# Bucketed attention and two feed-forward layers: another order of the first units, of the weight loads and of the drain

## The chip, the cores and the metric

One NeuronCore of one Trainium2 chip runs the whole kernel. The metric is the device time of one execution, in microseconds (us). The kernel before took 798.04 us, the median of three runs (796.69 to 798.05).

## What is computed

```python
# q, k, v: (2 batches, 8 heads, 768 tokens, 64), proj: (64, 6), all float32
q_bucket = sum((q @ proj > 0) * 2**bit); k_bucket likewise
scores = where(q_bucket == k_bucket, q @ k.T / 8, -1e9)
attn = softmax(scores) @ v
x = attn, heads joined: 1536 tokens x 512
# twice: w_in (512, 2048), w_out (2048, 512); the weights arrive as float64
h = x @ w_in;  g = h * clip(h + 3, 0, 6) / 6;  x = g @ w_out       # first layer
h = x @ w_in2; g = h * tanh(softplus(h));      out = g @ w_out2    # second layer
```

## The kernel before

**Attention.** Two heads of a batch form a pair; there are 8 pairs. A unit is 128 queries of one head against its 768 keys, so a pair has 12 units, and there are NU = 96. `attention_step(n)` (L657) is called with n = 0, 2, 4, ... and works on three generations at once: the scores S of units n and n+1 (`emit_S`, L565, into the PSUM tiles s0 and s1), the transposes T of units n-6 and n-5 (`emit_T`, L607, into the banks t0 and t1) and the product with V of units n-12 and n-11 (`emit_pv`, L626). TensorE gets them in the order PV, PV, T, S, T, S. Between S and T a unit passes through a minimum over its keys on VectorE (L581), the exponential on ScalarE (L587), four small statistics for four units together (L592, in every second step) and the normalization on GpSimd (L604). Each half of a transpose is taken out of its bank by ScalarE (L468) or VectorE (L469) before the next transpose may use that bank.

**A pair's preparation.** Scores need each operand in a high and a low float32r part, and the bucket bits as 12 more rows. The first pair is prepared straight into place (`k_hi`, `k_lo`, `q_hi`, `q_lo`, `q_dup`, `bits_out`, with `first_z` for the bucket products of TensorE), partly ahead of step 0 and partly in `late_prep` (L545), which is called right after step 0. A later pair p is prepared in stages by `prep(p, s)` (L476) at the ends of the steps of the pair before: the bucket products (`prep_z`, L425), the high parts kh and qh on GpSimd (L486), the scaled bits on GpSimd (L487) and the low part of q on VectorE (L489), then copies by DMA (`move`, L471) into the operand tiles KA, QA, QB, KX, the low part of k on GpSimd (L505) with its copies, and the load of pair p+1. For the second pair (p = 1) every stage stands one step later.

**Weights.** A weight unit is 512 KB of float64, loaded into one of five buffers (`w_load`, L104) and decoded into two float32r parts by some ten VectorE and ScalarE operations (L125 to L168) that `w_push` spreads over three calls. The first five loads are issued after step n = 4. The first decoding operation is a ScalarE one (L135) in step n = 18.

**Drain.** From n = 96 there are no more scores. The last six steps hold the last transposes (n = 96, 98 and 100) and products with V; after each step come the first matmuls of the feed-forward layer (`moe_pe(i)`: h of block i, and y of block i-2), two `w_push` calls, and the parts of g of a block (`g_parts`, L271: a ReLU on ScalarE, the gate on VectorE, the high part on ScalarE, the low part on VectorE) as hooks of one of the two. After the drain the rest of the kernel is 128 blocks of h and y, in which TensorE never stops.

**What sets the order.** The schedule is written by hand (`tc.manual_schedule()`): each engine executes its instructions in the order in which the program emits them, and all DMAs are issued by one queue, that of SyncE (SP), in that order too. A semaphore wait of one instruction holds up whatever stands behind it on its engine.

Of the kernel before, what the change touches and what calls it, by code (L numbers as in the profile page):

```python
# [20 lines left out]
def bucket_attention_two_moe_kernel(  # L21
# [208 lines left out]
    def w_push(u, hooks=()):  # L230
        w_slot(u, *w_pipe, hooks)
        w_pipe[:] = [u, w_pipe[0]]
# [4 lines left out]
    with tc.manual_schedule():  # L237
# [131 lines left out]
        with ExitStack() as actx:  # L369
# [23 lines left out]
            def load(p):  # L393
                if p < NPAIR:
                    b, hp = divmod(p, H // 2)
                    for nm, src in (("k", k), ("q", q)):
                        t = qk_p.tile([128, S], F32R, tag=nm, name=nm)
                        nc.sync.dma_start(out=t.bitcast(F32), in_=src[b, 2 * hp:2 * hp + 2].rearrange("h d s -> (h d) s"))
                        raw_t[p, nm] = t
# [71 lines left out]
            def move(dst, src):  # L471
                nc.sync.dma_start(out=dst.bitcast(F32), in_=src.bitcast(F32))

            def prep(p, s):  # L476
                s -= p == 1
                i = p % 2
                hd = [slice(0, 64), slice(64, 128)]
                if s == 0:  # L480
                    prep_z(p)
                elif s == 1:
                    kr, qr = raw_t[p, "k"], raw_t[p, "q"]
                    hi_t[p] = [qk_p.tile([128, S], F32R, tag=f"{nm}h", name=f"{nm}h") for nm in "kq"]
                    for t, r, c in zip(hi_t[p], (kr, qr), (1.0, -0.125)):
                        G.tensor_scalar(out=t, in0=r.bitcast(F32), scalar1=c, scalar2=1.0, op0=ALU.mult, op1=ALU.mult)  # L486
                    G.tensor_scalar(out=bit_t[p], in0=bit_t[p].bitcast(F32), scalar1=kbig, scalar2=1.0,  # L487
                                    op0=ALU.mult, op1=ALU.mult)
                    V.scalar_tensor_tensor(out=qr, in0=qr.bitcast(F32), scalar=-0.125, in1=hi_t[p][1].bitcast(F32),  # L489
                                           op0=ALU.mult, op1=ALU.subtract)  # L490
                    for h in range(2):
                        move(KA[i][h][lo_], hi_t[p][0][hd[h]])
                        move(KA[i][h][hi_], hi_t[p][0][hd[h]])
                        move(QB[i][h][lo_], hi_t[p][1][hd[h]])
                        move(QA[i][h][lo_], hi_t[p][1][hd[h]])
                elif s == 2:
                    for h in range(2):
                        for g in range(4):
                            hf, c = divmod(g, 2)
                            move((KX, QB)[c][i][h][64:64 + NZ, hf * HALF:(hf + 1) * HALF],  # L500
                                 bit_t[p][32 * g:32 * g + NZ, h])
                        move(QA[i][h][hi_], raw_t[p, "q"][hd[h]])
                elif s == 3:
                    kr = raw_t[p, "k"]
                    G.tensor_tensor(out=kr, in0=kr.bitcast(F32), in1=hi_t[p][0].bitcast(F32), op=ALU.subtract)  # L505
                    for h in range(2):
                        move(KX[i][h][lo_], kr[hd[h]])
                elif s == 4:
                    load(p + 1)


            A.preload_act_table_set("natural_log_exp_and_others")
# [26 lines left out]
            bits_out(0, "q", 0)  # L539
            q_hi(0, 1, G)  # L540
            k_lo(0, 1)
            q_lo(0, 1)
            load(1)

            def late_prep():  # L545
                for part in [first_z(hf, 1, ("t0", "t1")[hf]) for hf in range(2)]:
                    part()
                q_dup(0, 1)
                load_v(0)
                load_v(1)  # L550
                bits_out(0, "k", 1)
                bits_out(0, "q", 1)


            L = 6
# [98 lines left out]

            def attention_step(n, w_act=(), w_dve=()):  # L657
                u = n - L
                m = n - (L + 6)
                live = n < NU  # L660
                for k in (m, m + 1):
                    if 0 <= k < NU:
                        emit_pv(k // 6, k % 6)
                for k in range(2):
                    if 0 <= u + k < NU:
                        emit_T(u + k)
                    if live:
                        emit_S(n + k)
                out_now = m >= 0 and m % 6 == 4
                evac = 0 <= u < NU  # L670
                if evac:
                    emit_tevac(u, 0, acp)
                if out_now:
                    emit_pv_hi(m // 6)
                for part in w_act:
                    part()
                if evac:
                    emit_tevac(u, 1, vcp)
                if n % 4 == 0 and 0 < n <= NU:
                    emit_stats(n // 4 - 1)  # L680
                    for i in range(n - 4, n):
                        emit_norm(i)
                if live:
                    emit_min(n)
                if evac:
                    emit_tevac(u + 1, 0, acp)
                if live:
                    emit_exp(n)
                if evac:
                    emit_tevac(u + 1, 1, vcp if n // 2 % 6 in (0, 3, 4) and live else acp)  # L690
                if live:
                    emit_min(n + 1)
                    emit_exp(n + 1)
                if out_now:
                    emit_pv_lo(m // 6)
                    if m // 6 % 2 == 1 and m // 12 + 2 < NPAIR:
                        load_v(m // 12 + 2)
                if live:
                    for p in (n // 12, n // 12 + 1):
                        if 0 < p < NPAIR:  # L700
                            prep(p, n // 2 - 6 * (p - 1))
                for part in w_dve:
                    part()

# [8 lines left out]
            for n in range(0, NU, 2):  # L713
                attention_step(n, *w_at.get(n // 2, ((), ())))
                if n == 0:
                    late_prep()
                if n == 4:
                    for u in range(RAW):
                        w_load(u)
            qctx.close()  # L720
            more = ctx.enter_context(tc.tile_pool(name="more", bufs=1, reuse_waits="tile"))
            gp["g"] = ctx.enter_context(tc.tile_pool(name="g", bufs=2, reuse_waits="tile"))
# [1 line left out]
            for f in range(PRE, PRE + HERE):  # L724
                new_wslot(more, f)

            drain = (("h0", "g0"), ("h1", "g1"), ("", ""), ("h2", "g2"), ("h3", "g3"), ("h4", ""))
            u = 2 * PRE
            for n in range(NU, NU + L + 6, 2):
                attention_step(n)  # L730
                for part in drain[(n - NU) // 2]:
                    hooks = ()
                    if part[:1] == "h":
                        moe_pe(int(part[1]))
                    if part[:1] == "g":
                        hooks = g_parts(int(part[1]))
                    w_push(u, hooks)
                    u += 1

        last_w = ctx.enter_context(tc.tile_pool(name="lastw", bufs=1, reuse_waits="tile"))  # L740
# [46 lines left out]
```

## Time and profile before

| | us |
|---|---|
| median of 3 runs | 798.04 (796.69 to 798.05) |
| the profiled execution | 797.59 |
| its span, first to last instruction | 795.4 |
| TensorE (PE) busy | 764.8 (96%) |
| VectorE (DVE) busy | 491.9 (62%) |
| ScalarE (ACT) busy | 423.7 (53%) |
| GpSimd (POOL) busy | 134.1 (17%) |

The profile belongs to one execution. Its time is 2.2 us more than its span and 0.45 us less than the median. PE is the TensorE matmul row, PEld its weight loads, SPq the queue of SyncE that issues the DMAs. "Granted clock" is the share of TensorE's full clock that the throttle gave in a stretch.

### The profile page before, as it was taken

What the parts mean: (1) busy time and instruction counts of PE and PEld (TensorE: products, weight loads), DVE (VectorE), ACT (ScalarE), POOL (GpSimd) and SP (SyncE); (2) the same over time, 40 slices, a digit from 0 to 9 for tenths busy, and PEclk for the clock granted to TensorE, in tenths of its full rate; (3) what the DMA queues carried; (4) which work ended last, traced back from release to release, by engine and by line L of the source; (5) the groups of instructions that cost most, each with busy time, mean ns of one, the idle gap of its engine ahead of it and who ended that gap; (6) DMA issues with size and microseconds to landing.
All of it is one profiled execution on the core that took longest, in us unless ns stands there. A gap on an engine that the chain in (4) does not pass through costs nothing.

```text
span 795.4 us, 10531 instructions
## 1 busy us (share of the span) xinstructions
PE 764.8 (96%) x3776; PEld 590.5 (74%) x3776; DVE 491.9 (62%) x904; ACT 423.7 (53%) x787; POOL 134.1 (17%) x134
## 2 busy tenths in 40 slices
PE   6759999999998899999999999999999999999997
PEld 3637667666665578888888888888888888888886
DVE  5627778877888896756675676857565655121211
ACT  4427768677776886656455464555354444222221
POOL 2535655666544000000000000000000000000000
PEclk9979999999999899999999999999999999999999
DMA  4556447454600342212112121212112200010001
GB/s 139 142 168 150 110 123 194 112 150 140 147 28 27 132 138 101 79 56 78 53 63 71 53 80 54 80 54 80 54 54 78 81 26 1 1 53 1 32 22 54
DMA packets 22868, 64.77 MB, mean 81 GB/s; under 512 B 3840, under 2 KB 4512, under 8 KB 22816
## 3 DMA queue, kind: packets, MB, share of 16 engines
q1 hardware_dynamic: 22816, 64.10, 26.5%
q8 instruction: 30, 0.49, 0.3%
q14 instruction: 22, 0.18, 0.1%
HBM read 43.39 MB, written 3.15 MB: 59 GB/s over the span
## 4 chain that ended last, share of the span: by engine, by line
PE 91%; DVE 4%; DMA 2%; ACT 1%; POOL 1%; issue 1%; SPq 0%; DVEq 0%; ACTq 0%; POOLq 0%
PE s L310 33%; PE t L259 16%; PE pv L259 8%; PE t L618 8%; PE s L573 8%; PE m L259 8%; PE m L631 4%; PE pv L631 3%; DMA raw<-in_moe_w_in_dram 1%; PE m L432 1%; PE s L259 1%; DVE st L581 1%; DVE pt L469 1%; POOL p L604 0%; DMA kb<-k 0%
## 5 line engine op out<-in xcount | busy, mean ns | idle before, releaser
L291 DVE TENSOR_TENSOR gl<-gr,gh 128x512 fp32r<-128x512 f32 x96 | 66.2, 689 | 118.1 <-PE s L310 111.7
L604 POOL TENSOR_SCALAR p<-p,st 128x768 f32<-128x768 f32 x96 | 98.9, 1045 | 96.9 <-PE t L618 63.2
L587 ACT ACTIVATE p<-s,st 128x768 f32<-128x768 f32 x96 | 86.8, 904 | 38.6 <-DVE st L581 37.0
L581 DVE TENSOR_REDUCE st<-s 128x1 f32<-128x768 f32 x96 | 91.5, 954 | 24.0 <-PE s L573 20.8
L618 PEld LDWEIGHTS t<-ident,p 128*128 128x128 f32 x576 | 65.7, 144 | 45.7 <-issue 20.6
L618 PE MATMUL t<-ident,p 128*128 128x128 f32 x576 | 86.3, 286 | 11.0 <-DVE pt L469 5.7
L287 ACT CAST gh<-gr 128x512 fp32r<-128x512 f32 x96 | 59.7, 622 | 65.7 <-PE s L310 47.6
L468 ACT COPY pt<-t 128x384 f32<-128x384 f32 x121 | 57.6, 477 | 44.4 <-PE t L618 43.7
L259 PE MATMUL t<-xh,wih 128*128 128x512 f32 x192 | 75.0, 391 | 0.0
L259 PE MATMUL t<-xl,wih 128*128 128x512 f32 x192 | 74.7, 389 | 0.0
L259 PE MATMUL t<-xh,wil 128*128 128x512 f32 x192 | 74.7, 389 | 0.0
L310 PE MATMUL s<-gh,woh 128*128 128x512 f32 x192 | 74.7, 389 | 0.0
L310 PE MATMUL s<-gh,wol 128*128 128x512 f32 x192 | 74.7, 389 | 0.0
L310 PE MATMUL s<-woh,gh 128*128 128x512 f32 x192 | 74.7, 389 | 0.0
L310 PE MATMUL s<-wol,gh 128*128 128x512 f32 x192 | 74.7, 389 | 0.0
L573 PE MATMUL s<-ka,qa 128*128 128x384 f32 x192 | 60.7, 399 | 5.3 <-DMA qb<-bits 4.8
L573 PE MATMUL s<-kb,qb 76*128 76x384 f32 x192 | 53.3, 361 | 4.3 <-DMA kb<-k 3.8
L469 DVE COPY pt<-t 128x384 f32<-128x384 f32 x71 | 39.3, 554 | 27.8 <-PE t L618 27.7
L139 DVE SCALAR_TENSOR_TENSOR raw<-raw 128x512 uint32<-128x512 uint32 x64 | 44.1, 689 | 18.7 <-ACT raw L135 18.7
L310 PE MATMUL s<-woh,gl 128*128 128x512 f32 x192 | 51.8, 389 | 0.0
L310 PE MATMUL s<-gl,woh 128*128 128x512 f32 x192 | 51.3, 389 | 0.0
L157 ACT ACTIVATE raw<-raw 128x512 f32<-128x512 uint32 x64 | 43.1, 673 | 0.4 <-DVE raw L139 0.4
(126 smaller groups left out, 1431.7 us busy)
## 6 DMA issues: line engine op xcount, KB each, us to landing
raw<-in_moe_w_in_dram SPq DMA_DIRECT2D x32, 512.0 KB
raw<-in_moe_w_out_dram SPq DMA_DIRECT2D x32, 512.0 KB
ka<-kh SPq DMA_DIRECT2D x28, 192.0 KB
vn<-in_v_dram SPq DMA_DIRECT2D x8, 384.0 KB
out_dram<-yp SPq DMA_DIRECT2D x12, 256.0 KB
k<-in_k_dram SPq DMA_DIRECT2D x7, 384.0 KB
q<-in_q_dram SPq DMA_DIRECT2D x7, 384.0 KB
qb<-qh SPq DMA_DIRECT2D x14, 192.0 KB
```

Of the source, the lines that this page charges most:

```text
L259: P.matmul(ps, lhsT=w[:, cs], rhs=x[t][:, c, :], start=(n == 0), stop=(n == 3 * KB - 1))
L287: A.copy(new_g(i)[0], gr_t[i])
L291: V.tensor_tensor(out=gl, in0=gr_t.pop(i), in1=gh.bitcast(F32), op=ALU.subtract)
L310: P.matmul(ys[d // 2][:, d % 2, :], lhsT=w, rhs=g, start=(j == 0 and part == 0 and n == 0), stop=(j == NH - 1 and part == 1))
L468: acp = lambda o, i: A.copy(o, i)
L469: vcp = lambda o, i: V.tensor_copy(o, i)
L573: P.matmul(ps[:, hf, :HALF], lhsT=w[rr, qs], rhs=m[rr, hf * HALF:(hf + 1) * HALF], start=(w is QA[i][h]), stop=(w is QB[i][h]))
L581: V.tensor_reduce(out=st_t[n // 4][:, 0, n % 4:n % 4 + 1], in_=s_t[n][:, :, :HALF], op=ALU.min, axis=AX.XY)
L587: A.activation(out=pt, in_=s_t.pop(n)[:, :, :HALF], func=AF.Exp, scale=-1.0, bias=st[:, 0, n % 4:n % 4 + 1], accum_out=st[:, 1, n % 4:n % ...
L604: G.tensor_scalar(out=p_t[n], in0=p_t[n], scalar1=st[:, 3, i:i + 1], scalar2=st[:, 4, i:i + 1], op0=ALU.mult, op1=ALU.add)
L618: P.transpose(ps[:, i * 128:(i + 1) * 128], src[:, hf, i * 128:(i + 1) * 128], ident)
L631: P.matmul(pv_t[gi][64 * h:64 * h + 64, :HALF], lhsT=vn_t[p][:, h, j, :], rhs=pt_t[gi, h][j // 3][:, j % 3, :], start=(j == 0), stop=(j == ...
```

## The change

Four edits. (1) The second pair's stages are one step earlier or more: kh and qh and their eight copies are issued at the end of `late_prep`, right after step 0; the scaled bits come with the bucket products in step 2, the copies of the bits and the low part of q in step 4, the low part of k in step 6, the load of the third pair in step 8. For later pairs the stages keep their steps, and only the order inside a stage differs. (2) The five first weight loads leave step 4 and are issued one at a time after steps 14, 16, 18, 20 and 22; the load of the second pair's V moves from `late_prep` to step 8. (3) `q_lo(0, 1)`, the low part of q of the first pair's second head, moves on VectorE from ahead of step 0 to behind it. (4) In the drain, `moe_pe(h)` is emitted by `mid`, between the transposes of the step's two units instead of after the step (in the last three steps there are no transposes, and the order on TensorE is the same), and the parts of g go with the first of the two `w_push` calls instead of the second.

```diff
@@ -473,40 +473,56 @@
+            hd = [slice(0, 64), slice(64, 128)]
+
+            def prep_hi(p):
+                i = p % 2
+                hi_t[p] = [qk_p.tile([128, S], F32R, tag=f"{nm}h", name=f"{nm}h") for nm in "kq"]
+                for t, nm, c in zip(hi_t[p], "kq", (1.0, -0.125)):
+                    G.tensor_scalar(out=t, in0=raw_t[p, nm].bitcast(F32), scalar1=c, scalar2=1.0,
+                                    op0=ALU.mult, op1=ALU.mult)
+                for h in range(2):
+                    move(KA[i][h][lo_], hi_t[p][0][hd[h]])
+                    move(KA[i][h][hi_], hi_t[p][0][hd[h]])
+                for h in range(2):
+                    move(QB[i][h][lo_], hi_t[p][1][hd[h]])
+                    move(QA[i][h][lo_], hi_t[p][1][hd[h]])
+
+            def prep_scale(p):
+                G.tensor_scalar(out=bit_t[p], in0=bit_t[p].bitcast(F32), scalar1=kbig, scalar2=1.0,
+                                op0=ALU.mult, op1=ALU.mult)
+
+            def prep_bits(p):
+                for h in range(2):
+                    for g in range(4):
+                        hf, c = divmod(g, 2)
+                        move((KX, QB)[c][p % 2][h][64:64 + NZ, hf * HALF:(hf + 1) * HALF],
+                             bit_t[p][32 * g:32 * g + NZ, h])
+
+            def prep_q_lo(p):
+                qr = raw_t[p, "q"]
+                V.scalar_tensor_tensor(out=qr, in0=qr.bitcast(F32), scalar=-0.125, in1=hi_t[p][1].bitcast(F32),
+                                       op0=ALU.mult, op1=ALU.subtract)
+
+            def prep_q_move(p):
+                for h in range(2):
+                    move(QA[p % 2][h][hi_], raw_t[p, "q"][hd[h]])
+
+            def prep_k_lo(p):
+                kr = raw_t[p, "k"]
+                G.tensor_tensor(out=kr, in0=kr.bitcast(F32), in1=hi_t[p][0].bitcast(F32), op=ALU.subtract)
+                for h in range(2):
+                    move(KX[p % 2][h][lo_], kr[hd[h]])
+
+
+            PREP = ((prep_z,), (prep_hi, prep_scale, prep_q_lo), (prep_bits, prep_q_move), (prep_k_lo,),
+                    (lambda p: load(p + 1),), ())
+            PREP1 = ((), (prep_z, prep_scale), (prep_bits, prep_q_lo, prep_q_move), (prep_k_lo,),
+                     (lambda p: load(p + 1),), ())
+
             def prep(p, s):
-                s -= p == 1
-                i = p % 2
-                hd = [slice(0, 64), slice(64, 128)]
-                if s == 0:
-                    prep_z(p)
-                elif s == 1:
-                    kr, qr = raw_t[p, "k"], raw_t[p, "q"]
-                    hi_t[p] = [qk_p.tile([128, S], F32R, tag=f"{nm}h", name=f"{nm}h") for nm in "kq"]
-                    for t, r, c in zip(hi_t[p], (kr, qr), (1.0, -0.125)):
-                        G.tensor_scalar(out=t, in0=r.bitcast(F32), scalar1=c, scalar2=1.0, op0=ALU.mult, op1=ALU.mult)
-                    G.tensor_scalar(out=bit_t[p], in0=bit_t[p].bitcast(F32), scalar1=kbig, scalar2=1.0,
-                                    op0=ALU.mult, op1=ALU.mult)
-                    V.scalar_tensor_tensor(out=qr, in0=qr.bitcast(F32), scalar=-0.125, in1=hi_t[p][1].bitcast(F32),
-                                           op0=ALU.mult, op1=ALU.subtract)
-                    for h in range(2):
-                        move(KA[i][h][lo_], hi_t[p][0][hd[h]])
-                        move(KA[i][h][hi_], hi_t[p][0][hd[h]])
-                        move(QB[i][h][lo_], hi_t[p][1][hd[h]])
-                        move(QA[i][h][lo_], hi_t[p][1][hd[h]])
-                elif s == 2:
-                    for h in range(2):
-                        for g in range(4):
-                            hf, c = divmod(g, 2)
-                            move((KX, QB)[c][i][h][64:64 + NZ, hf * HALF:(hf + 1) * HALF],
-                                 bit_t[p][32 * g:32 * g + NZ, h])
-                        move(QA[i][h][hi_], raw_t[p, "q"][hd[h]])
-                elif s == 3:
-                    kr = raw_t[p, "k"]
-                    G.tensor_tensor(out=kr, in0=kr.bitcast(F32), in1=hi_t[p][0].bitcast(F32), op=ALU.subtract)
-                    for h in range(2):
-                        move(KX[i][h][lo_], kr[hd[h]])
-                elif s == 4:
-                    load(p + 1)
+                for part in (PREP1 if p == 1 else PREP)[s]:
+                    part(p)
             A.preload_act_table_set("natural_log_exp_and_others")
@@ -539,17 +555,17 @@
             bits_out(0, "q", 0)
             q_hi(0, 1, G)
             k_lo(0, 1)
-            q_lo(0, 1)
             load(1)
             def late_prep():
+                q_lo(0, 1)
                 for part in [first_z(hf, 1, ("t0", "t1")[hf]) for hf in range(2)]:
                     part()
                 q_dup(0, 1)
-                load_v(0)
-                load_v(1)
                 bits_out(0, "k", 1)
                 bits_out(0, "q", 1)
+                load_v(0)
+                prep_hi(1)
             L = 6
@@ -654,7 +670,7 @@
-            def attention_step(n, w_act=(), w_dve=()):
+            def attention_step(n, w_act=(), w_dve=(), mid=lambda: None):
                 u = n - L
                 m = n - (L + 6)
                 live = n < NU
@@ -666,6 +682,8 @@
                         emit_T(u + k)
                     if live:
                         emit_S(n + k)
+                    if k == 0:
+                        mid()
                 out_now = m >= 0 and m % 6 == 4
                 evac = 0 <= u < NU
                 if evac:
@@ -696,9 +714,8 @@
                     if m // 6 % 2 == 1 and m // 12 + 2 < NPAIR:
                         load_v(m // 12 + 2)
                 if live:
-                    for p in (n // 12, n // 12 + 1):
-                        if 0 < p < NPAIR:
-                            prep(p, n // 2 - 6 * (p - 1))
+                    if n // 12 + 1 < NPAIR:
+                        prep(n // 12 + 1, n // 2 % 6)
                 for part in w_dve:
                     part()
@@ -714,9 +731,10 @@
                 attention_step(n, *w_at.get(n // 2, ((), ())))
                 if n == 0:
                     late_prep()
-                if n == 4:
-                    for u in range(RAW):
-                        w_load(u)
+                if n == 8:
+                    load_v(1)
+                if 14 <= n < 14 + 2 * RAW:
+                    w_load(n // 2 - 7)
             qctx.close()
             more = ctx.enter_context(tc.tile_pool(name="more", bufs=1, reuse_waits="tile"))
             gp["g"] = ctx.enter_context(tc.tile_pool(name="g", bufs=2, reuse_waits="tile"))
@@ -724,17 +742,13 @@
             for f in range(PRE, PRE + HERE):
                 new_wslot(more, f)
-            drain = (("h0", "g0"), ("h1", "g1"), ("", ""), ("h2", "g2"), ("h3", "g3"), ("h4", ""))
+            drain = ((0, 0, None), (1, 1, None), (None, None, None), (2, 2, None), (3, 3, None), (4, None, None))
             u = 2 * PRE
             for n in range(NU, NU + L + 6, 2):
-                attention_step(n)
-                for part in drain[(n - NU) // 2]:
-                    hooks = ()
-                    if part[:1] == "h":
-                        moe_pe(int(part[1]))
-                    if part[:1] == "g":
-                        hooks = g_parts(int(part[1]))
-                    w_push(u, hooks)
+                h, *gs = drain[(n - NU) // 2]
+                attention_step(n, mid=lambda: h is not None and moe_pe(h))
+                for g in gs:
+                    w_push(u, () if g is None else g_parts(g))
                     u += 1
         last_w = ctx.enter_context(tc.tile_pool(name="lastw", bufs=1, reuse_waits="tile"))
```

## Rows read from the trace of the kernel before

**Rows 1.** Busy time by stretch: start:end, length, busy us (count) by engine, granted clock, DMA.

```profile
30.00:40.00 10.00, 7.90 (x40) 6.97 (x41) 8.02 (x15) 5.18 (x11) 4.12 (x5) 1.00 1.00 270
43.50:58.95 15.45, 6.66 (x31) 3.66 (x31) 3.52 (x8) 2.64 (x6) 5.55 (x6) 0.67 0.42 115
63.28:80.76 17.48, 17.48 (x115) 12.18 (x116) 13.46 (x25) 14.13 (x32) 10.13 (x9) 1.00 0.55 146
```

**Rows 2.** Timeline, opening: start, us, engine, line, instruction, count, [idle before <-releaser].

```profile
11.04 0.98 PE L573 MATMUL s<-kb,qb 76*128 76x384 f32 x2 [0.48 <-ACT qb L445]
...
11.39 2.56 DVE L455 SCALAR_TENSOR_TENSOR qa<-q,qb 64x768 fp32r<-64x768 f32 x1 [0.72 <-POOL qb L451]
13.98 1.82 DVE L581 TENSOR_REDUCE st<-s 128x1 f32<-128x768 f32 x2
...
18.56 0.98 PE L573 MATMUL s<-kb,qb 76*128 76x384 f32 x2
...
23.12 3.89 POOL L604 TENSOR_SCALAR p<-p,st 128x768 f32<-128x768 f32 x4 [5.13 <-DVE st L598]
...
24.16 1.54 PE L618 MATMUL t<-ident,p 128*128 128x128 f32 x6 [0.30 <-POOL p L604]
...
28.65 1.66 DVE L489 SCALAR_TENSOR_TENSOR q<-q,qh 128x768 fp32r<-128x768 f32 x1 [3.79 <-POOL qh L486]
...
30.83 0.90 PE L618 MATMUL t<-ident,p 128*128 128x128 f32 x3 [3.20 <-DVE pt L469]
31.38 0.99 PE L573 MATMUL s<-ka,qa 128*128 128x384 f32 x2
```

**Rows 3.** Timeline, units 10 to 13: transposes, copies, and who waits for them.

```profile
39.75 0.84 PE L618 MATMUL t<-ident,p 128*128 128x128 f32 x6 [1.06 <-ACT pt L468]
...
48.36 0.68 PE L573 MATMUL s<-ka,qa 128*128 128x384 f32 x2 [4.82 <-DMA qb<-bits]
...
49.56 1.17 SPq L472 DMA_DIRECT2D kb<-k  x2
52.82 0.98 PE L573 MATMUL s<-kb,qb 76*128 76x384 f32 x2 [3.78 <-DMA kb<-k]
...
53.52 0.33 SPq L398 DMA_DIRECT2D k<-in_k_dram  x1
...
56.55 0.84 PE L432 MATMUL m<-k,pz 64*32 64x384 f32 x1 [0.19 <-DMA k<-in_k_dram]
```

**Rows 4.** Timeline of TensorE: first products with V of steps 14, 24 and 26.

```profile
58.95 1.51 PE L631 MATMUL pv<-pt,vn 128*64 128x384 f32 x8
...
80.69 1.51 PE L631 MATMUL pv<-pt,vn 128*64 128x384 f32 x8
...
86.35 1.51 PE L631 MATMUL pv<-pt,vn 128*64 128x384 f32 x8
```

**Rows 5.** Timeline of SyncE's queue: first and last of pair 3's 20 copies.

```profile
89.08 1.11 SPq L472 DMA_DIRECT2D ka<-kh  x2
...
102.59 1.17 SPq L472 DMA_DIRECT2D kb<-k  x2
```

**Rows 6.** Timeline of ScalarE, step 18 (the same columns).

```profile
70.21 0.71 ACT L135 ACTIVATE raw<-raw 128x512 uint32<-128x512 uint32 x1
```

**Rows 7.** Timeline, drain: ends of the transposes' waits and the clock behind them.

```profile
255.37 0.52 PE L618 MATMUL t<-ident,p 128*128 128x128 f32 x3 [1.25 <-ACT pt L468]
...
257.23 0.90 PE L618 MATMUL t<-ident,p 128*128 128x128 f32 x3 [1.34 <-DVE pt L469]
...
266.34 0.55 DVE L469 COPY pt<-t 128x384 f32<-128x384 f32 x1
...
267.62 2.83 PE L631 MATMUL m<-pt,vn 128*64 128x384 f32 x8
```

**Rows 8.** Timeline of VectorE: the same multiplication beside GpSimd's normalization and alone.

```profile
223.70 1.36 DVE L162 TENSOR_TENSOR wil<-raw,wih 128x512 fp32r<-128x512 f32 x1
...
257.09 0.68 DVE L162 TENSOR_TENSOR wil<-raw,wih 128x512 fp32r<-128x512 f32 x1
```

## The prediction

> **What bounds the kernel now.** I read the busy time by stretch first. From 63 us on TensorE is busy all the time, 17.48 of 17.48 us, while VectorE and ScalarE are at 77% and 81% and GpSimd at 58%; between 43.5 and 58.95 it is busy for 6.66 of 15.45 us, at a granted clock of 0.67 [rows 1]. So in the middle only TensorE counts, and what the change can give lies at the two ends: the opening, up to the first product with V of step 14 at 58.95 [rows 4], and the drain. Whatever moves that instant moves everything behind it by as much, as long as the saturated part stays as it is. The timeline of the opening then names TensorE's stalls. A first one of 3.20 us: the second half of a transpose waits for VectorE's copy, which stands on VectorE behind the low part of q of pair 1, which has waited 3.79 us for the high part, which stands on GpSimd behind four normalizations of 3.89 us [rows 2]. A second of 4.82 us: unit 12 waits for the operand copies of pair 1, queued behind the five weight loads of step 4 (2.5 MB). A third of 3.78 us: the same unit waits for the copy of k's low part, issued only at 49.56 [rows 3]. The sum is 11.8 us. Then comes a low clock: three half transposes take 0.90 us in the opening [rows 2] and 0.52 us at 255.37 [rows 7]. The granted-clock column says 1.00 for 30 to 40 us, but the durations are those of the lower level (1.2 GHz) until about 35.5, where TensorE had been busy since 30.83; after the two long stalls they are so again until 58.95.
>
> **The opening, step by step.** I replay the order with durations of the rows.
>
> (a) `q_lo(0,1)` takes 2.56 us on VectorE at 11.39, and the first two minima follow at 13.98 [rows 2]. The first unit's scores end at 12.0 (11.04 + 0.98 [rows 2]), so the minimum can start there; both minima (1.82) are done at about 14.2, `q_lo` then runs alone in 0.95 (the same line's other instruction), and the first two exponentials end by 15.2, ahead of `q_dup`. Unit 3 no longer waits for its operands: its last product starts at about 17.7 instead of 18.56 [rows 2]. Gain 0.9 to 1.0 us. The cover is TensorE's own `first_z`, which lasts to 16.0; without it `q_lo` would delay unit 3 by at most its 0.95.
>
> (b) Pair 1's kh and qh now stand on GpSimd behind `bits_out`, at 17.5 to 19.1, where it idles, and the scaling of the bits (0.90) at 21.2 to 22.1, just ahead of the normalizations. These begin at about 22.15 instead of 23.12, and the first transpose at 23.15 instead of 24.16 [rows 2]: still 1.0 us gained, with the scaling already in it.
>
> (c) The low part of q now comes on VectorE at about 23.8, behind the minimum of unit 5, with its input long there. It runs beside the four normalizations. The nearest row for a two-input operation beside these is 1.36 us, against 0.68 alone [rows 8]; the same low part took 1.66 beside the scaling [rows 2]. I take 1.7, between 0.95 alone and the end of the whole series (22.15 + 3.89 + its own 0.95 = 27.0, which would cost 1.2 us here): copy at 25.5 to 26.0, second half of the transpose at 26.4 (it follows the first half) instead of 30.83. Gain so far 4.4. The Trainium skill (SBUF — State Buffer, "SBUF: two separate sides") speaks against this place: it says that a VectorE operation with two SBUF inputs and a GpSimd operation shut each other out for a whole instruction. By it the normalization under way is waited for once; the trace agrees as far as 1.36 is more than 0.68 and less than a normalization's 0.97 on top of it, and the sum stays.
>
> (d) Steps 8 and 10 have no product with V; here the lookahead of two units sets the pace, not TensorE. Before, unit 10's second transpose waited 1.06 us for ScalarE [rows 3], and the chain is minimum 0.95, exponential 0.90 + 0.19, copy 0.48, transpose. At the higher clock from about 29 on, my replay puts unit 7's scores at 27.0, unit 8's at 28.8, unit 9's at 31.5, unit 10's at 33.0, unit 11's at 35.9 and the products with V of step 12 at 36.9, instead of 41.22 (two steps of some 4.2 each, as before). At the lower clock throughout, a unit costs some 2.56 us of TensorE and step 12 begins at 39.1.
>
> (e) Step 12 finds its operands: pair 3's 20 copies took SyncE 14.7 us (89.08 to 103.8 [rows 5]), 0.74 each; the eight copies of (b) are issued from 18.4, so to 24.3, the eight of bits and two of q to 31.7, the two of k's low part, which GpSimd has ready by 28.8, to 33.2, and lands by 36.2 (before: issued 49.56, waited for until 52.82 [rows 3]). Needed at 39.5. The load of pair 2 waits for that copy, goes out at 36.3 and lands 3.0 us later, as 53.52 to 56.55 [rows 3], so 39.3; its bucket products come at 41.2. Both stalls and the wait for this load go, by 2 to 3 us of slack. A step with bucket products lasts 5.66 us (80.69 to 86.35 [rows 4]), so step 14 starts at 36.9 + 5.66 = 42.6 instead of 58.95: **16.4 us**. Cross-check by what is removed: 3.2 + 4.8 + 3.8, plus 1.0 from (a), plus some 3.5 for the stretch 52.8 to 58.95 at the low clock (6.1 us for what takes 2.6 at the high one) is 16.3.
>
> **The moved weight loads.** Each of the five is now issued in SyncE's queue behind the stage of its step. That queue is busy in these steps: pair 3's copies go out without a break from 89.08, 2.7 us after the start of their step 26 at 86.35, to 103.8 [rows 4, 5]. The first load goes out after eight copies, 2.7 + 5.9 = 8.6 us after the start of step 14, and 0.5 MB at the 270 GB/s of 30 to 40 us [rows 1] is 1.9 us; with the latency and the copies ahead of it I estimate that it lands 12 to 13.5 us after that start. ScalarE's first use, in order ahead of two exponentials, comes 70.21 - 58.95 = 11.3 us after it [rows 4, 6]. So ScalarE stalls 1 to 2 us there once, and TensorE, with two units ahead of it, loses 0 to 1.5; I take 0.7. The second load delays the last copies of pair 2 by 2 to 3 us. They would be out 17.4 us after the start of step 14 (as 103.8 against 86.35) and are needed at about 24.7: covered by some 4 us. The load of V moves to step 8 and is needed at step 24: nothing.
>
> **The drain.** h0 goes between the transposes of step 96 and covers the copies of the first unit (0.4 us gained), and h1 does so in step 98. Before, step 98's second transpose waited 1.25 for ScalarE and then 1.34 for VectorE [rows 7], and h1 ran after it, its first half at the low clock. After: h1 ends at about 256.2, under these waits. But the decoding that ScalarE did during h0 before now stands behind copies that wait for the second transpose, which waits for h0: ScalarE idles 3 us there, VectorE with it. VectorE's chain then runs from the ReLU at 252 through nine operations (4.5 to 5 us), a copy at 257.3 to 257.8, the next ReLU at 259.4, and 13 operations (6.5 us) to the copy for the last transpose at 265.9, against 266.34 [rows 7]. So of 4 us hidden under h1 only 0.4 is left: VectorE is late next. TensorE idles about 4.5 us in one piece ahead of the last transpose, and the clock, low there before as well (eight products with V took 2.83 instead of 1.51 [rows 7]), may stay low 0 to 1.7 us longer. Net: 0, between 1 gained and 3 lost.
>
> **Sum**, against the profiled execution: 797.59 - 16.4 + 0.7 + 0 = 781.9. The median lies 0.45 above that execution, so 782.3.
>
> **The rivals.** (1) The clock does not come up in steps 6 to 12. For: short gaps remain there, and 19.5 to 27.6 ran at the low level although TensorE was mostly busy. Against: it rose within 5 us of work without gaps after 30.83. Then step 12 begins at 39.1 and lasts about 7.9, step 14 at 47.0: 12 us gained, 786.5. (2) The drain loses: low clock after the 4.5 us of idling, or VectorE's chain with GpSimd's contention a microsecond longer: 3 us, 785.3. (3) The weight loads hold up pair 2: as the copies of pair 1 came behind the loads before, those of pair 2 may now, and unit 24 waits; beyond the 4 us of cover each microsecond counts, I price it at 3: 785. (4) **Slower than before**: the lower clock holds on in the saturated part, since TensorE now enters it from steps with gaps. At the low level a step costs 8 us instead of 4.35, so 3.6 per step; from the fifth such step after step 14 on, the 16 us are gone, and eight steps give 811. Against: saturated steps kept the high level, with a granted clock of 1.00 [rows 1]. (5) The stalls stay, because something else in the queues (the wait of pair 2's load on the copies, say) holds pair 1's copies: 798. Against: every input of these copies is there by 29.
>
> **Chances.** Forecast, 779 to 785: 0.66. (1) 0.13, (2) 0.10, (3) 0.06, (4) 0.03, (5) 0.02. The range 778 to 789 takes in the first four with their bounds (best: 17.2 in the opening, 1 in the drain, no stall, 779; worst: (1) with 2 us from (2)). A difference of 0.2% (1.6 us) is about what a measurement of this kernel can tell. Faster 0.95, same 0.02, slower 0.03.
>
> **What would show it.** The first product with V of step 14 near 42.6; no wait on the copies of qb or kb in the opening; no stall of three microseconds at the second transpose; full clock by about 30; ScalarE waiting for a DMA at L135 in step 18; the last transpose within 1 us of where it was, relative to step 14, and a longer idle time of TensorE ahead of it. I am wrong if step 14 begins after 47, if unit 24 waits for a DMA, or if the distance from step 14 to the first h of the third block changes by over 3 us.

## The result

The changed kernel takes 784.29 us, the median of 4 runs (782.89 to 785.34), beside 797.37 us (796.01 to 798.05, 4 runs) of the kernel before: a ratio of 0.984, 95% interval 0.981 to 0.986. The forecast was 782.3 us in a range of 778 to 789, with 0.95 on faster. The profiled execution has a span of 781.1 us, 14.3 us less than before; its time, 782.89 us, is the lowest of the four.

Five instants of TensorE split a span: the first product with V of the steps 14, 26, 96 and 104, and the end. Each number below is the difference of two starts in the timeline of that kernel's profile.

| us | to step 14 | 14 to 26 | 26 to 96 | 96 to 104 | 104 to the end | span |
|---|---|---|---|---|---|---|
| before | 58.95 | 27.40 | 159.24 | 30.54 | 519.27 | 795.4 |
| changed | 42.59 | 29.72 | 159.19 | 30.31 | 519.29 | 781.1 |
| forecast (changed) | 42.6 | 28.1 | as before | as before | as before | 779.7 |

The opening gives 16.36 us, 2.32 of which are lost again by step 26, and the drain gives 0.23. Everything else is unchanged to 0.1 us, as a part that TensorE's own work fills should be.

The opening of the changed kernel, TensorE's timeline (start, us, instruction, count, idle time before it and its releaser). These lines answer to [rows 2 to 4].

```profile
11.59 0.98 PE L589 MATMUL s<-kb,qb 76*128 76x384 f32 x2 [0.77 <-DVE kb L442]
...
20.71 0.62 PE L589 MATMUL s<-ka,qa 128*128 128x384 f32 x2
...
24.40 1.54 PE L634 MATMUL t<-ident,p 128*128 128x128 f32 x6 [1.95 <-POOL p L620]
...
27.01 1.01 PE L634 MATMUL t<-ident,p 128*128 128x128 f32 x6
...
35.46 0.85 PE L634 MATMUL t<-ident,p 128*128 128x128 f32 x6 [1.06 <-ACT pt L468]
...
36.94 1.51 PE L647 MATMUL pv<-pt,vn 128*64 128x384 f32 x8
...
42.59 1.51 PE L647 MATMUL pv<-pt,vn 128*64 128x384 f32 x8
```

The stalls of 3.20, 4.82 and 3.78 us are gone; the wait of 1.06 us for ScalarE's copy in step 10, which the replay counted as the pace of steps 8 and 10, is there to the hundredth. One wait is new: the first transpose now stands 1.95 us for GpSimd, 0.30 before. TensorE was already at the high clock ahead of it (two products of scores in 0.62 us at 20.71, 1.01 us in the kernel before) and worked at the low one behind it, until 27.7.

What was lost stands in the timelines of SyncE, ScalarE and TensorE in steps 14 to 20, and in the busy times of steps 18 and 20 (columns as in [rows 1]):

```profile
45.32 2.39 SPq L472 DMA_DIRECT2D ka<-kh  x4
...
50.76 0.70 SPq L109 DMA_DIRECT2D raw<-in_moe_w_in_dram  x1
```

```profile
57.14 0.66 ACT L135 ACTIVATE raw<-raw 128x512 uint32<-128x512 uint32 x1 [3.17 <-DMA raw<-in_moe_w_in_dram]
```

```profile
58.30 0.85 PE L634 MATMUL t<-ident,p 128*128 128x128 f32 x6 [1.21 <-ACT pt L468]
```

```profile
51.22:55.59 4.37, 4.37 (x30) 3.00 (x29) 3.31 (x6) 2.63 (x6) 4.37 (x5) 1.00 0.97 228
55.59:61.94 6.35, 4.77 (x30) 3.03 (x29) 3.55 (x9) 4.61 (x10) 1.85 (x3) 1.00 0.51 118
```

The first weight load leaves 8.2 us after the start of step 14 and lands 14.5 us after it (ScalarE starts at 57.14); the DMA engines are busy 0.97 of step 18, with this load and the copies around it. ScalarE reaches L135 at 54.0, waits 3.17 us, and step 20 lasts 6.35 us instead of 4.31. This answers to [rows 6], where L135 did not wait. That is 2.0 of the 2.3 us. Step 24 adds 0.4, 6.06 us instead of 5.66: TensorE's bucket products wait 0.26 us for k and 0.28 us for q of pair 3 (PEld row, 70.56 and 71.51).

The drain of the changed kernel, TensorE and VectorE, for [rows 7]:

```profile
250.94 0.88 PE L634 MATMUL t<-ident,p 128*128 128x128 f32 x3 [4.37 <-ACT pt L468]
252.55 0.90 PE L634 MATMUL t<-ident,p 128*128 128x128 f32 x3 [0.73 <-DVE pt L469]
253.38 2.83 PE L647 MATMUL m<-pt,vn 128*64 128x384 f32 x8
```

```profile
238.40 0.69 DVE L283 SCALAR_TENSOR_TENSOR gr<-gr,s 128x512 f32<-128x512 f32 x1 [3.43 <-ACT gr L277]
...
245.47 0.69 DVE L283 SCALAR_TENSOR_TENSOR gr<-gr,s 128x512 f32<-128x512 f32 x1 [1.14 <-ACT gr L277]
...
251.95 0.55 DVE L469 COPY pt<-t 128x384 f32<-128x384 f32 x1
```

### The profile page after: what moved, and what is told of

Same layout as the page of the kernel before. It is cut to its first block, busy times and chain, and to the rows that moved or that the text cites. A ratio compares the mean times of both kernels' runs of the same rounds, so it can differ in the third digit from the quotient of the medians.

```text
span 781.1 us, 10534 instructions
## 1 busy us (share of the span) xinstructions
PE 757.3 (97%) x3776; PEld 585.7 (75%) x3776; DVE 490.0 (63%) x904; ACT 423.5 (54%) x787; POOL 134.0 (17%) x134
## 3 DMA queue, kind: packets, MB, share of 16 engines
HBM read 43.39 MB, written 3.15 MB: 60 GB/s over the span
## 4 chain that ended last, share of the span: by engine, by line
PE 92%; DVE 4%; ACT 1%; DMA 1%; issue 1%; SPq 0%; POOL 0%; DVEq 0%; ACTq 0%; POOLq 0%
PE s L310 33%; PE t L259 17%; PE pv L259 8%; PE t L634 8%; PE m L259 8%; PE s L589 8%; PE m L647 4%; PE pv L647 4%; DVE st L597 1%; PE m L432 1%; DMA raw<-in_moe_w_in_dram 1%; ACT p L603 1%; DVE pt L469 0%; PE t L432 0%; PE m L418 0%
## 5 line engine op out<-in xcount | busy, mean ns | idle before, releaser
L634 PE MATMUL t<-ident,p 128*128 128x128 f32 x576 | 84.3, 282 | 12.8 <-ACT pt L468 8.4
L589 PE MATMUL s<-ka,qa 128*128 128x384 f32 x192 | 58.7, 388 | 0.5 <-DVE qa L455 0.5
L589 PE MATMUL s<-kb,qb 76*128 76x384 f32 x192 | 51.3, 349 | 0.8 <-DVE kb L442 0.8
L135 ACT ACTIVATE raw<-raw 128x512 uint32<-128x512 uint32 x64 | 42.8, 669 | 3.2 <-DMA raw<-in_moe_w_in_dram 3.2
```

The source lines that it names most:

```text
L589: P.matmul(ps[:, hf, :HALF], lhsT=w[rr, qs], rhs=m[rr, hf * HALF:(hf + 1) * HALF], start=(w is QA[i][h]), stop=(w is QB[i][h]))
L634: P.transpose(ps[:, i * 128:(i + 1) * 128], src[:, hf, i * 128:(i + 1) * 128], ident)
```

## The experiments

Two theories were open after the result. One: the opening's gain needs both the early stages and the moved loads, the loss of 2.3 us is the late first load, and the drain only moves its waits. The rivals: one of the parts did it all, the loss has another cause, or the drain gave or took something that this profile hides. The table has what each profile showed; times are medians of n runs beside 796.68 us (9 runs, first four kernels), 797.45 us (9, next four) and 797.38 us (9, last two) of the kernel before.

| us | time (n) | ratio, 95% | to step 14 | 14 to 26 | 26 to 96 | 96 to 104 |
|---|---|---|---|---|---|---|
| old_drain | 785.29 (5) | 0.983 to 0.987 | 43.25 | 32.70 | 159.23 | 29.13 |
| load0_early | 783.75 (5) | 0.982 to 0.986 | 42.08 | 28.73 | 159.24 | 30.35 |
| loads_only | 791.71 (4) | 0.992 to 0.995 | 52.64 | 28.04 | 159.23 | 30.72 |
| prep_only | 789.84 (4) | 0.990 to 0.994 | 51.40 | 27.40 | 159.24 | 30.45 |
| spaced | 781.96 (4) | 0.979 to 0.982 | 42.08 | 27.41 | 159.23 | 30.66 |
| drain_between | 781.47 (5) | 0.979 to 0.982 | 43.37 | 31.12 | 159.26 | 27.13 |
| best | 777.81 (4) | 0.974 to 0.977 | 43.42 | 27.41 | 159.27 | 25.81 |
| qlo_front | 785.26 (1) | | 44.13 | 30.64 | 159.27 | 30.12 |
| best_pool | 776.97 (5) | 0.972 to 0.976 | 42.32 | 27.40 | 159.28 | 27.14 |
| best_again | 778.37 (4) | 0.973 to 0.978 | 41.87 | 27.41 | 159.32 | 24.76 |

### The two parts of the opening, each alone

**loads_only**: the kernel before, with step 4's loads removed and issued after steps 14 to 22 (`if 14 <= n < 14 + 2 * RAW: w_load(n // 2 - 7)`), V's load in step 8.

> The kernel before with the moved weight loads alone (and the load of V at step 8). Theory, the parts share the gain: the stall of 3.2 us at the second transpose stays, that of 4.8 us at unit 12 goes and that on k's low part shrinks to 1 or 2 us; step 14 starts near 49.5, then 2.3 us go at step 18: 790. Rival, the weight loads were all of it: step 14 near 45, 786. Other rival, late preparation was all of it: 797.

**prep_only**: the kernel before, with the changed stages of `prep` and `prep_hi(1)` at the end of `late_prep`, all else as before, except that the loads of V stand behind the two `bits_out` of `late_prep`.

> The kernel before with the earlier stages of the second pair alone (weight loads after step 4). Theory: no stall at the second transpose, but k's low part is copied behind the five loads and lands at 42 to 44, and the load of pair 2 behind it: two waits of some 3 us in step 12, step 14 near 48.5, no wait in step 18: 788. Rival, the early copies are enough and the loads do no harm behind them: step 14 at 43.6, 783.

Step 14 came at 52.64 and 51.40. Each alone gives 6.3 and 7.6 us of the 16.4, so neither was all of it, and the opening needs both. That 6.3 and 7.6 add up to less than 16.4 does not show that the parts help each other: the executions did not start alike (unit 0's second product at 12.69, 11.45 and 11.59, at 11.04 before). Counted from that product, the way to step 14 shrinks from 47.91 us to 39.95, 39.95 and 31.00: 8.0 and 8.0 apart, 16.9 together, which is hardly more than the sum. The stalls expected were there, and step 14 still came 3 us later than expected in both. With the loads alone, the transpose still waits behind the low part of q (4.10 us here) and k's low part still arrives late, TensorE's timeline:

```profile
31.79 0.90 PE L617 MATMUL t<-ident,p 128*128 128x128 f32 x3 [4.10 <-DVE pt L469]
```

```profile
46.66 0.59 PE L572 MATMUL s<-kb,qb 76*128 76x384 f32 x2 [1.66 <-DMA kb<-k]
```

With the early stages alone step 12 begins at 36.79, as in the changed kernel (36.94), so the gain up to there is theirs alone. Then TensorE stands: the copy of k's low part is issued at 36.45 behind the five loads, and unit 12 starts 9 us later. TensorE's row names no releaser; that it is this copy follows from SyncE, whose next load waits for the same copy and leaves at 46.02. It is one wait of 6.04 us where two of some 3 us were expected. SyncE's queue, TensorE, and the granted clock (0.63) of the stretch behind the stall:

```profile
36.45 1.11 SPq L472 DMA_DIRECT2D kb<-k  x2
46.02 0.33 SPq L398 DMA_DIRECT2D k<-in_k_dram  x1
```

```profile
45.49 0.98 PE L590 MATMUL s<-kb,qb 76*128 76x384 f32 x2 [6.04 <-issue]
```

```profile
46.00:53.00 7.00, 6.82 (x37) 3.47 (x36) 3.62 (x5) 2.40 (x5) 1.78 (x3) 0.63 0.59 164
```

The missing 3 us are mostly this clock: from unit 12's second half to step 14 it took 5.9 us here and 6.0 in loads_only (42.59 - 39.44 = 3.15 in the changed kernel), with a wait of 0.2 and 0.5 us for pair 2's load in it. The expectation had the stall, and not the work at the lower clock that follows it. And without the loads between 14 and 22, the stretch to step 26 is 27.40 again: the loss of 2.3 us belongs to the loads. They do not cost it everywhere, though. In loads_only they stand in the same places, 2.3 us were expected there too, and the stretch is only 0.6 longer: the copies of pair 2 start before step 14, the first load leaves 4.4 us after its start (57.01) and not 8.2, and ScalarE starts L135 at 64.53 without a wait. In time, then, the parts add up and no more: their medians are 5.0 and 6.8 us below the kernel before, that of old_drain (below), which has both, 11.4.

### Where the loads should stand

**load0_early**: the changed kernel with

```diff
-                if 14 <= n < 14 + 2 * RAW:
-                    w_load(n // 2 - 7)
+                if n in (12, 16, 18, 20, 22):
+                    w_load((12, 16, 18, 20, 22).index(n))
```

> The changed kernel with the first weight load after step 12 instead of step 14, the other four as they are. Theory, ScalarE's wait of 3.2 us in step 18 costs TensorE the 2.3 us by which steps 14 to 26 are longer: no such wait, 27.4 to 27.8 us from step 14 to step 26 instead of 29.7, time 782. Rival, the five loads' traffic among the copies of pair 2 is what costs: unchanged at 784.

ScalarE's wait is gone and steps 14 to 24 last 21.74 us, five of 4.35. But step 24 takes 6.99 instead of 5.66: the load of pair 3 waits for the last copies of pair 2, which are issued between the second and the third weight load, leaves 7.7 us after them, and the bucket products wait for it.

```profile
53.32 0.72 ACT L135 ACTIVATE raw<-raw 128x512 uint32<-128x512 uint32 x1
```

```profile
58.33 1.10 SPq L472 DMA_DIRECT2D kb<-k  x2
59.47 0.59 SPq L109 DMA_DIRECT2D raw<-in_moe_w_in_dram  x1
66.05 0.34 SPq L398 DMA_DIRECT2D k<-in_k_dram  x1
```

```profile
69.08 0.51 PE L432 MATMUL m<-k,pz 64*32 64x384 f32 x1 [0.88 <-DMA k<-in_k_dram]
```

So theory and rival were each half right: two costs, of which ScalarE's wait had hidden most of the second (1.3 us here, 0.4 in the changed kernel). The medians, 783.75 and 784.29, do not differ by more than their runs do.

**spaced**: the same edit with `(12, 22, 24, 34, 36)`, where SyncE's queue is empty and the decoding still comes later.

> The changed kernel with the five first weight loads after steps 12, 22, 24, 34 and 36, where SyncE's queue is empty, instead of 14 to 22. Theory, both costs of the loads are gone, ScalarE's wait at L135 and the late load of pair 3 behind the copies of pair 2: 27.4 us from step 14 to step 26, no low clock there, 781.5 with less spread from run to run. Rival, the loss between the steps 14 and 26 is not the loads': 784.

27.41 us, as before the change, and 781.96 us: both costs gone. The spread of the runs, 2.4 us, is no less than that of the changed kernel.

### The drain

**old_drain**: the changed kernel with the drain of before.

> The changed kernel with the drain of before (edit 4 undone). Theory, the new drain moves waits but not its end: 22 us from the first product with V of step 96 to that of step 102 in either order, time within 1 us of the changed kernel (784). Rival, the new drain is worth something that the run of the profile hides: 3 us slower (787), or 3 us faster (781) if it costs.

From step 96 to step 102 it took 20.40 us here, from 96 to 104 29.13, against 22.03 and 30.54 of the same order in the kernel before, and 30.45 and 30.72 of it in the two kernels above; the new order shows 30.1 to 30.7 in the four profiles that have it. The 20.40 is the clock again: from the last half transpose of step 98 to the next product with V the same work took 3.2 us here and 4.7 us in the kernel before, where it began at the low level. So the new drain is worth nothing that stands out from the clock's scatter, and 785.29 beside 784.29 is no difference either. The profile shows more: after ScalarE's wait for the first load, the clock fell in this execution, and step 22, with no wait in it, lasted 6.09 us instead of 4.42.

```profile
56.23:64.20 7.97, 6.00 (x29) 4.09 (x29) 3.63 (x9) 5.11 (x11) 3.10 (x4) 0.80 0.56 142
64.20:70.29 6.09, 6.09 (x29) 3.80 (x29) 3.41 (x4) 2.60 (x7) 1.46 (x2) 0.69 0.74 169
```

That is 5.3 us lost between steps 14 and 26, against 2.3 in the changed kernel's profile, for a wait of ScalarE of 3.55 us against 3.17. drain_between and qlo_front, with the same loads and waits of 3.42 and 3.52 us, lost 3.7 and 3.2: nearly the same wait costs one execution up to twice what it costs another.

**drain_between**: the changed kernel, with `attention_step` calling `between()` after the copies and statistics of a step's first unit, and

```diff
-            drain = ((0, 0, None), (1, 1, None), (None, None, None), (2, 2, None), (3, 3, None), (4, None, None))
+            drain = ((0, (None, None), ()), (1, (0,), (None,)), (None, (), (1, None)),
+                     (2, (), (2, None)), (3, (), (3, None)), (4, (), (None, None)))
+                h, first, after = drain[(n - NU) // 2]
+                attention_step(n, mid=lambda: h is not None and moe_pe(h), between=lambda: push(first))
+                push(after)
```

> The changed kernel with the decoding of the drain's first units put between the copies of the two units of a step, so that VectorE and ScalarE work while TensorE runs h0 and h1 (two weight units in step 96, one in step 98; the parts of g one step later). Theory, the drain is bounded by VectorE's and ScalarE's chains, and the 3.4 us in which VectorE waits for the first ReLU are what can be had: the last transpose comes about 4 us sooner, without the low clock behind it, 30.3 us from step 96 to step 104 become 25 to 26, time 779. Rival, the chains only move and the work comes due later: 784.

From 96 to 102 it takes 18.0 us instead of 21.9, as expected; the low clock behind it stayed (eight products in 2.83 us), so 96 to 104 is 27.13, not 25 to 26. VectorE's first long wait is gone.

```profile
249.86 0.87 PE L634 MATMUL t<-ident,p 128*128 128x128 f32 x3 [2.15 <-ACT pt L468]
250.91 0.90 PE L634 MATMUL t<-ident,p 128*128 128x128 f32 x3 [0.18 <-DVE pt L469]
251.74 2.83 PE L647 MATMUL m<-pt,vn 128*64 128x384 f32 x8
```

**best**: both edits, spaced loads and decoding between.

> Both of these together. Theory, the two ends do not touch each other and the gains add: 776 to 777. Rival, the decoding of the drain takes back what the loads give: 779.

777.81 us, a ratio of 0.976 (0.974 to 0.977): faster than both kernels, if 0.8 us short of what was expected. The gains add: 2.3 us for spaced and 2.8 for drain_between against the changed kernel, 6.5 for both. The 1.3 us on top are as much as the clock made in the drain between two profiles (25.81 us here, 27.13 in drain_between).

### The first units

**qlo_front**: the changed kernel with `q_lo(0, 1)` ahead of step 0 again.

> The changed kernel with the low part of q of the first pair's second head back ahead of step 0 (edit 3 undone). Theory, the first minimum waits behind it and unit 3 with it: step 14 starts 1.0 us later, at 43.6. Rival, TensorE's own work ahead of unit 2 covers it: step 14 at 42.6 as in the changed kernel.

Step 14 came at 44.13, but this execution can't be read against 42.59: unit 0's second product starts at 12.83 here and at 11.59 there. Counted from it, the first transpose, at 25.70 here and 24.40 there, comes after 12.87 us against 12.81, and after 12.79 in prep_only, which also has `q_lo` ahead. So up to there edit 3 is worth nothing, and the rival held. To step 14 it is 31.30 us against 31.00, and 30.5 to 30.9 in the seven other profiles with `q_lo` behind: that difference arises only behind the first transpose, where some executions work at the low clock and others not. The timelines of GpSimd, VectorE and TensorE show what happened ahead of it:

```profile
10.47 1.80 POOL L465 TENSOR_TENSOR kb<-k,ka 64x768 fp32r<-64x768 f32 x1
10.48 2.20 DVE L442 TENSOR_SCALAR kb<-bits 12x768 fp32r<-12x768 f32 x1
12.61 0.94 DVE L455 SCALAR_TENSOR_TENSOR qa<-q,qb 64x768 fp32r<-64x768 f32 x1
12.83 0.98 PE L589 MATMUL s<-kb,qb 76*128 76x384 f32 x2 [1.90 <-DVE kb L442]
13.61 0.84 PE L589 MATMUL s<-ka,qa 128*128 128x384 f32 x2
13.84 0.96 DVE L597 TENSOR_REDUCE st<-s 128x1 f32<-128x768 f32 x1 [0.29 <-PE s L589]
```

VectorE's `bits_out`, 0.55 us in the kernel before, is held for 2.20 us, and `q_lo` then runs while TensorE still works for the first minimum. In the kernel before it was `q_lo` that was held (2.56 us). Which of the two it is depends on when GpSimd gets q: its q_hi starts between 9.1 and 10.4 us in the ten profiles so far, and where it starts by 9.43 (five of them), k_lo starts just ahead of `bits_out`.

**best_pool** and **best_again**, on the same chip: best with `bits_out(0, "k", 0, G)` instead of `V`, and best as it is.

> The kernel of both (weight loads in empty places, decoding under h0 and h1) with one more edit: the first head's k bits (L442) go on GpSimd, ahead of its q_hi and k_lo, instead of on VectorE. Theory, the 1.3 us between the openings of the runs (step 14 at 42.1 or at 43.4) come from VectorE's 0.55 us operation being held for 2.20 us when GpSimd's k_lo starts just ahead of it, which depends on when the load of q lands: no wait of TensorE for L442, unit 0's second product at 11.3, step 14 near 42.1 in every run, 777 with less spread. Rival, GpSimd, busy then, is late with k_lo: step 14 at 43 or later, 778.5.

> The kernel of both once more, on the same chip as the run with the bits on GpSimd: 777.8 again, with unit 0's second product at 11.3 or at 12.8 by the landing of q. If both runs agree within their spread, the place of the bits is worth less than a run can tell.

On GpSimd the operation takes 0.83 us and unit 0's second product starts at 11.38, after a wait of 0.56 us for it; in best_again VectorE was not held (0.55 us) and the product started at 11.41. Step 14 came at 42.32 and 41.87, so the rival, a late k_lo, did not show. 776.97 (775.53 to 778.08) and 778.37 (775.4 to 779.3) lie within each other's runs: whether the edit is worth the half microsecond that it should be on average stays open.

```profile
10.50 0.83 POOL L442 TENSOR_SCALAR kb<-bits 12x768 fp32r<-12x768 f32 x1 [3.06 <-DVE bits L409]
```

The same places in best_again, VectorE and GpSimd:

```profile
10.48 0.55 DVE L442 TENSOR_SCALAR kb<-bits 12x768 fp32r<-12x768 f32 x1
10.49 2.21 POOL L465 TENSOR_TENSOR kb<-k,ka 64x768 fp32r<-64x768 f32 x1
```

best_again's profile is also the one in which the clock never fell in the drain: 24.76 us from 96 to 104 for the instructions that took 25.81 in best. Not all of it is kept: behind step 104 best_again takes 520.24 us and best 519.49, and at 276.50 its TensorE waits 0.62 us for ScalarE's high part of g, a wait that best does not have there. So the rival of drain_between, that the work comes due later, shows in part in this profile, whose drain is the shortest. Busy time and granted clock of steps 100 and 102 in best, then TensorE's timeline in best_again:

```profile
241.38:248.10 6.72, 4.07 (x22) 2.12 (x21) 6.69 (x15) 5.62 (x13) 0.00 (x0) 0.85 0.44 136
248.10:255.91 7.81, 7.81 (x34) 5.17 (x33) 6.77 (x15) 7.71 (x14) 0.00 (x0) 0.91 0.31 97
```

```profile
245.78 0.55 PE L634 MATMUL t<-ident,p 128*128 128x128 f32 x3 [0.51 <-DVE pt L469]
246.25 1.51 PE L647 MATMUL m<-pt,vn 128*64 128x384 f32 x8
```

## Why the prediction was right, and where it was off

**The opening** (16.4 forecast, 16.36 found) was read from the right view: the three stalls by their releasers, and behind them the lower clock. That is the mechanism, and it held. That the number came out to 0.04 us is luck: single steps missed and made up for each other. (a) gained nothing here, not 1.0: unit 3's last products start at 18.57, 18.56 before. `bits_out` was now held by GpSimd (1.08 us), and `q_lo` ahead cost nothing even in qlo_front. (b) had the first transpose at 23.15; it came at 24.40, later than before. The scaling of the bits, which stands ahead of the normalizations, began at 22.34 and not at 21.2, behind a wait for VectorE, whose last operation on those bits ended at 22.2, and it ended at 23.24. Beside it the last statistic that the normalizations wait for took 0.69 us instead of 0.16, to the same end. GpSimd and VectorE:

```profile
22.34 0.90 POOL L492 TENSOR_SCALAR bits<-bits,kbig 128x768 fp32r<-128x768 f32 x1 [2.42 <-DVE st L612]
22.56 0.69 DVE L614 SCALAR_TENSOR_TENSOR st<-st 128x4 f32<-128x4 f32 x1
```

(c) was 1.20 us, not 1.7 (the four normalizations around it took 4.58 us, 3.89 before), and the second transpose ran from 27.01 on without a gap. (d) took this up: steps 8 and 10 go at the pace of the chain through VectorE and ScalarE, and the clock was up again at 27.7, not from about 29 on. So from the first transpose to step 12 it took 12.54 us where the replay had 13.75, and the 1.25 us lost by (a) and (b) were back: step 12 came at 36.94 for 36.9, step 14 at 42.59 for 42.6. (e) held, with pair 1's last copies issued at 32.39.

The cross-check by what is removed agreed by luck as well. Its 1.0 from (a) was not there, and its 3.5 for the low clock was 3.0: the work behind the second stall takes 3.15 us at the high clock, not 2.6. It did not count what made up for both: 1.3 us more than the stall between the first transpose and step 12, where the clock was up at 27.7 instead of about 35.5, and 0.5 in step 12.

**The weight loads** were the term that was mis-sized: 0.7 forecast, 2.3 in the profile, 5.3 in another. The load left 8.2 us after the start of step 14 (8.6 forecast) and landed 14.5 us after it, not 12 to 13.5, and ScalarE waited 3.17 us, not 1 to 2. The estimate gave the load alone the 270 GB/s that in [rows 1] all transfers of a full stretch moved together, and 1.5 to 3 us for the latency and the 1.5 MB of copies ahead of it; but the DMA engines were busy for all of step 16 (1.00, 245 GB/s) and most of step 18 (0.97). The place and the mechanism were named. The second cost, pair 3's load behind the copies of pair 2, was not: the cover of 4 us was counted up to unit 24, and not up to the load that waits for the same copies (0.4 us here, 1.3 in load0_early).

**The drain** came out at 0.2 for a forecast of 0, by the chain given: VectorE's copy for the last transpose 20.45 us after the start of step 96 (20.3 forecast), and TensorE idle 4.37 us in one piece. drain_between showed that the idle time of VectorE and ScalarE under h0 (VectorE's 3.43 us) was the cause, since filling it brought step 102 3.9 us nearer to step 96.

**The rivals.** That the clock stays low, (1), held only for step 6, up to 27.7. Rival (3) happened in part, for pair 3's load instead of unit 24. The median, 784.29 for 782.3, is off by the loads (1.6 us) and by the profiled execution: it lies 1.4 us below the median, and the forecast took the distance of before (0.45). That would fit a clock behind the remaining stalls and a landing of q that differ from run to run, which the runs without a profile cannot show.

## What to carry to other kernels

In a kernel like this large prefetches belong where the issuing queue is empty, and the check is not only when their data is needed, but which transfers stand behind them and what waits for those. A stall of TensorE costs more than its own length whenever it brings the clock down, here by 2.8 us for the work behind a stall of 6.04 us (prep_only). Before two runs' openings are compared, the start of each has to be compared: here it alone was worth up to 1.8 us (11.04 to 12.83). Work moved ahead of a long instruction on TensorE helps only if the engines that wait for that instruction get other work to do meanwhile.

## What the runs showed of the hardware

A VectorE operation with one tensor input, the scaling of 12 rows of bits, is held by a GpSimd operation that started first, as one with two inputs is (`q_lo`, 2.56 us instead of 0.95 in the kernel before). It takes 2.20 us instead of 0.55 when GpSimd's two-input k_lo starts 0.01 to 0.02 us ahead of it (five profiles), 0.79 to 1.08 us where GpSimd's one-input q_hi has 0.4 to 0.7 us still to run (three profiles), and 0.55 us when k_lo starts 0.01 us behind it (best_again). Even a statistic of 128x4 numbers took 0.69 us instead of 0.16 beside a GpSimd operation. Whether q lands early or late thus puts unit 0's second product at 12.7 to 12.8 us or at 11.0 to 11.6.

The granted clock is not the same in two executions of one kernel: behind the same waits of the drain it stayed at 1.00 in best_again and fell to 0.85 and 0.91 in best, and the stretch from step 96 to 104 took 24.76 and 25.81 us.

A clock that comes up early can be lost again. In the changed kernel, prep_only and qlo_front TensorE was at the high level 9 to 10 us after unit 0's second product, then waited 1.7 to 1.95 us for the first normalization and worked at the low level until 27.6 to 29.7 (granted clock 0.52 from 24.0 to 27.5 us in the changed kernel). In the seven other profiles with the early stages it came up 10.7 us or more after that product, the wait was 1.0 to 1.3 us, and it stayed up; their step 12 came 24.8 us after the product, that of the three 25.3 to 25.6.
